# Attention and two dense layers on one core: narrower value weights, a new beginning, a new plan

## The chip, the core and the metric

The kernel runs on one core of a Trainium2 chip. The metric is the device time of one execution in microseconds (us). A core has TensorE (PE: matrix products; PEld in a profile is its weight load), VectorE (DVE), ScalarE (ACT), GpSimd (POOL) and SyncE (SP), which here issues nearly all transfers. Each engine works through its own queue in order; they wait for each other by semaphores.

## The reference

Inputs are q, k, v of shape (2, 8, 768, 64), a projection of 64x6, and the weights of two dense blocks.

```python
q_bits = (einsum('bhsd,dk->bhsk', q, proj) > 0)      # 6 bits, the same for k
mask = q_bucket[:, :, :, None] == k_bucket[:, :, None, :]
scores = where(mask, 0.125 * q @ k.T, -1e9); scores -= max(scores, -1)
attn = exp(scores); attn = attn / (sum(attn, -1) + 1e-9)
x = (attn @ v) laid out as 1536 tokens x 512
x = max(0.01 * (x @ w_in), x @ w_in) @ w_out          # 512 -> 2048 -> 512
h = x @ w_in2; return (h * cos(h)) @ w_out2           # 512 -> 2048 -> 512
```

The dense weights arrive as 64-bit floats.

## The kernel before

Every operand of a product is split into a high part and a low rest, and a product is the sum of high x high, high x low and low x high. Attention goes head by head (16 of them, n), within a head by tiles of 128 keys (six, k). Pieces of a head, by the names of the code: `load` and `hi`/`lo` split q and k into a tile `at` (four in a ring, so `at_71` holds heads 3, 7, 11 and 15); `bm`/`bw` are the bits product (L277) and its write (L283); `mm`/`mr` the products for row maxima (L293) and their reductions (L299); `rt`/`fl`/`dr` turn the maxima into a row, finish it and send it by DMA into `at` (L303, L308, L313); `qk` are the score products (L370, L371), `ex`/`cv` two passes of ScalarE over them, which give the exponential and its high part `phi`, `sub` the low rest `plo` (L392, on VectorE or GpSimd); `pe`, `pv`, `pw` the value products (L397, L405), which add up in one PSUM tile `pv`; `ev` copies it out, `lc`, `rc`, `dw`, `rr`, `xm` divide by the sum (its reciprocal is L419, and `lc`, L416, is the small DMA ahead of it). A value product has 128 weight columns: 64 of v, and 64 that are ones (for the sum of the row) on the other side for odd heads. The sum of v over all keys (`sv`, L342, with 65 columns of ones) enters the correction for rows without a match.

After the maxima of head n the row of -1 that goes with them was sent into each `at` once by a DMA (L454).

The dense weights are turned from 64-bit to two 32-bit floats in pieces `w0` to `w6` (L588 to L592 and L581; VectorE, ScalarE, GpSimd). The first eight chunks of them are placed among the last heads, since their space becomes free then. The two dense layers follow in 96 steps; the first twelve are part of the plan, the rest is written out.

The order of work is computed when the kernel is built: `Plan.order` keeps a time for each engine, takes for each engine the piece that can start first (ties go to the lowest key: `KEY` per kind, `FIX` for a kind and a head, `CHUNK_KEY`), adds its cost from `COST`, and so on. The resulting list is issued as it stands; each engine's queue is its share of that list.

## Time and profile before

| | us |
|---|---|
| three runs, median (lowest, highest) | 791.51 (790.81, 791.82) |
| span of the profiled execution, first to last instruction | 789.9 |
| TensorE busy in it | 772.2 |
| VectorE, ScalarE, GpSimd busy | 472.9, 435.1, 408.9 |

The profiled execution's own device time isn't listed apart from its span; the runs lie 0.9 to 1.9 us above the span, which begins with the first instruction and ends with the last. Busy time on TensorE counts a product from its start to its modelled end, so records of neighbours overlap, and a sum of durations is more than the time that passes. In a timeline a row in brackets with "idle" tells how long the engine stood before that group, and what ended the wait.

### The profile page before, as it was taken

To read this page: it belongs to the slowest core of one execution; us is meant where nothing else is said; L and a number is where in the kernel's file an instruction comes from. 1 tells how busy PE (TensorE), PEld (TensorE's weight loads), DVE (VectorE), ACT (ScalarE), POOL (GpSimd) and SP (SyncE) were. 2 spreads that over 40 slices of the span, in tenths; PEclk is the share of its full clock that TensorE was granted. 3 is DMA by queue.
4 is the path that set the end of the run, shared out by engine and by line. 5 is a ranking of instruction groups with operands and counts; after the bars stand their busy time and mean duration, and the time that the engine had idled before them with its cause. 6 is when DMAs were issued, how large, how long until landed. Compare 5 with 4: busy or idle time off the path is not lost.

```text
span 789.9 us, 9962 instructions
## 1 busy us (share of the span) xinstructions
PE 772.2 (98%) x3660; PEld 666.1 (84%) x3660; DVE 472.9 (60%) x599; ACT 435.1 (55%) x630; POOL 408.9 (52%) x263
## 2 busy tenths in 40 slices
PE   5999999999998999999999999999999999999998
PEld 3999999999888888888888888888888888888886
DVE  6656777777597875256366275357546738743333
ACT  3687777877778744243243233366556645644432
POOL 8777675666575634255345346747615433532211
PEclk9999999999999999999999999999999999999999
DMA  6553543542613622032022013112203200000012
GB/s 179 134 129 84 147 96 92 137 104 65 197 32 132 219 107 107 1 107 90 18 107 75 32 54 108 53 41 75 98 1 107 107 1 1 0 1 1 0 54 107
DMA packets 24329, 63.20 MB, mean 80 GB/s; under 512 B 7596, under 2 KB 11620, under 8 KB 20184
## 3 DMA queue, kind: packets, MB, share of 16 engines
q1 hardware_dynamic: 24136, 62.43, 26.0%
q8 instruction: 29, 0.48, 0.3%
q14 instruction: 20, 0.16, 0.1%
q10 hardware_dynamic: 144, 0.13, 0.0%
HBM read 46.21 MB, written 3.19 MB: 63 GB/s over the span
## 4 chain that ended last, share of the span: by engine, by line
PE 92%; DVE 3%; ACT 2%; DMA 2%; issue 1%; POOL 0%; SPq 0%; DVEq 0%; ACTq 0%; POOLq 0%
PE h L664 33%; PE y L706 33%; PE pv L405 11%; PE st L293 4%; PE st L370 4%; PE st L371 4%; PE st L277 2%; PE st L342 1%; DMA raw<-in_qk_dram 1%; PE pv L397 1%; DMA sums<-yx 1%; DVE mx L299 0%; ACT st L385 0%; DVE wsc L591 0%; ACT phi L377 0%
## 5 line engine op out<-in xcount | busy, mean ns | idle before, releaser
L695 POOL TENSOR_TENSOR gl<-gf,gh 128x512 fp32r<-128x512 f32 x88 | 136.2, 1548 | 261.1 <-ACT gh L689 188.7
L706 PE MATMUL y<-gh,at 128*128 128x512 f32 x576 | 177.0, 388 | 0.0
L664 PE MATMUL h<-XH,at 128*128 128x512 f32 x576 | 142.3, 389 | 0.0
L664 PEld LDWEIGHTS h<-XH,at 128*128 128x128 f32 x576 | 108.1, 188 | 22.4
L706 PEld LDWEIGHTS y<-gh,at 128*128 128x128 f32 x576 | 108.0, 188 | 22.4
L299 DVE TENSOR_REDUCE mx<-st 128x1 fp32r<-128x768 f32 x96 | 90.3, 953 | 37.1 <-PE st L293 35.3
L706 PE MATMUL y<-gl,at 128*128 128x512 f32 x288 | 111.8, 388 | 0.0
L392 POOL TENSOR_TENSOR plo<-pf,phi 128x768 fp32r<-128x768 f32 x43 | 81.3, 1894 | 56.1 <-ACT phi L388 49.3
L671 ACT ACTIVATE gf<-h 128x512 f32<-128x512 f32 x48 | 28.7, 597 | 139.8 <-PE h L664 135.8
L681 DVE TENSOR_TENSOR gf<-h,gf 128x512 f32<-128x512 f32 x48 | 33.2, 691 | 108.2 <-ACT gf L671 108.0
L675 ACT ACTIVATE ki<-h 128x512 int32<-128x512 f32 x48 | 28.7, 598 | 105.1 <-PE h L664 105.1
L676 DVE SCALAR_TENSOR_TENSOR gf<-ki,h 128x512 f32<-128x512 int32 x48 | 33.0, 687 | 75.1 <-ACT ki L675 75.1
L664 PE MATMUL h<-XL,at 128*128 128x512 f32 x288 | 77.0, 389 | 0.0
L370 PE MATMUL st<-at 77*128 77x384 f32 x192 | 67.0, 349 | 3.3 <-DVE plo L392 1.3
L371 PE MATMUL st<-at 128*128 128x384 f32 x192 | 65.1, 339 | 0.0
L585 POOL TENSOR_TENSOR at<-wsc,at 128x1024 fp32r<-128x1024 f32 x24 | 59.1, 2462 | 9.6 <-ACT at L592 9.6
L664 PEld LDWEIGHTS h<-XL,at 128*128 128x128 f32 x288 | 54.1, 188 | 11.2
L706 PEld LDWEIGHTS y<-gl,at 128*128 128x128 f32 x288 | 54.0, 188 | 11.1
L689 ACT ACTIVATE gh<-gf 128x512 fp32r<-128x512 f32 x96 | 60.0, 625 | 3.0 <-DVE gf L681 1.5
L706 PE MATMUL y<-gh,wx 128*128 128x512 f32 x192 | 58.7, 387 | 0.0
L685 DVE SCALAR_TENSOR_TENSOR gf<-gf,h 128x512 f32<-128x512 f32 x48 | 32.9, 686 | 41.7 <-ACT gf L684 41.7
L392 DVE TENSOR_TENSOR plo<-st,phi 128x768 fp32r<-128x768 f32 x53 | 50.3, 952 | 10.5 <-ACT st L385 9.1
(105 smaller groups left out, 1452.1 us busy)
## 6 DMA issues: line engine op xcount, KB each, us to landing
wrvh<-in_w_dram SPq DMA_DIRECT2D x16, 1024.0 KB
wrvl<-in_w_dram SPq DMA_DIRECT2D x16, 1024.0 KB
at<-at SPq DMA_DIRECT2D x63, 192.0 KB
raw<-in_qk_dram SPq DMA_DIRECT2D x15, 384.0 KB
vraw<-in_v_dram SPq DMA_DIRECT2D x4, 768.0 KB
yx<-dr SPq DMA_DIRECT2D x16, 192.0 KB
out_dram<-ys SPq DMA_DIRECT2D x6, 256.0 KB
out_dram<-yx SPq DMA_DIRECT2D x5, 256.0 KB
```

The lines of the kernel that those rows point to most:

```text
L299: V.reduce_max(mx[n][:, t:t + 1], mps.pop((n, t))[:, :, 0:HS], axis=AX.XY)
L370: T.matmul(o, at[0:R76 + 1, 2, kc], at[0:R76 + 1, 0, COL[h]], start=True, stop=False)
L371: T.matmul(o, at[:, 3, kc], at[:, 1, COL[h]], start=False, stop=True)
L392: (V if LO[n][k] == "V" else G).tensor_tensor(halves(plo[n, k]), pf.pop((n, k)), halves(f32(phi[n, k])), op=ALU.subtract)
L405: T.matmul(ot[n][:, h, 0:HS], w, x[:, COL[h]], start=False, stop=(k == C - 1 and part == 1))
L585: G.tensor_tensor(lf, sc, f32(hf), op=ALU.subtract)
L664: self.tc.nc.tensor.matmul(ps, w[:, 0, k], x[:, k, cols], start=(j == 0), stop=(j == 3 * KT - 1))
L676: nc.vector.scalar_tensor_tensor(g, ki, -TWOPI, ps, op0=ALU.mult, op1=ALU.add)
L681: nc.vector.tensor_tensor(g, ps, g, op=ALU.max)
L689: self.tc.nc.scalar.activation(gh, self.gs[s], AF.Copy)
L695: (nc.vector if s < GLV else nc.gpsimd).tensor_tensor(gl, g, f32(gh), op=ALU.subtract)
L706: self.tc.nc.tensor.matmul(self.half(e, c), w[:, 1, e], x[:, c], start=(j == 0 and i == 0), stop=(j == GRP - 1 and i == 2))
```

## The change

Value products get 65 weight columns: v's 64 and one of ones, so the sum always stands in row 64. The tiles `vh` and `vl` are laid out as 65 columns per head; the last factor of odd heads gets a tile of its own (`rr1`). The row of -1 comes as a 13th row with the key bits (threshold and weight in `cst`), and its four DMAs are gone. The signed projection is spread out on the host and finished by three VectorE steps; its two loads are issued by ScalarE. SyncE now issues the two halves of head 0, then v, then head 1. Clearing of `e` and `sv` goes from GpSimd to VectorE. `Plan` gets a second kind of dependence (`behind`: after a piece's start), a latency per engine apart from the cost (`TAIL`), other costs and other keys. 70 pieces `un` with the lowest priority are put on TensorE: each is a product of `ones` and `e0` into the first value tile, which nobody reads; the plan takes one where nothing else can start.

```diff
-    load=-181, hi=20, d2=-40, d3=51, lo=-43, dl=-14, bm=-37, bw=7, db2=-47, db1=-61, mm=-8, mr=34, rt=-30,
+    load=1353.52, hi=10.36, d2=366, d3=385.48, lo=1205.02, dl=-630.48, bm=-1032.92, bw=280.97, db2=-59.3,
...
-    mm=0.351, mr=0.953, rt=0.12, fl=0.55, dr=0.75, de=1.3, neg=0.65, qk=0.702, ex=0.81, cv=0.84, subV=0.95, subG=1.87,
+    mm=0.349, mr=0.87, rt=0.06, fl=0.43, dr=0.78, de=1.55, qk=0.704, ex=0.705, cv=0.735, subV=0.875, subG=1.81,
...
+TAIL = dict(P=0.16, V=0.09, A=0.1, G=0.05, Q=0.0)
+COLD = 7.0
+UNREAD = 70
...
-            if e == "P" and t < 22:
+            if e == "P" and t < COLD:
                 c *= 1.9
...
+            for o in it["behind"]:
+                o["left"] -= 1
+                o["at"] = max(o.get("at", 0.0), t)
+                if o["left"] == 0:
+                    ready[o["e"]].append(o)
+            end = t + c + TAIL[e]
...
-        SV = [con.tile([128, 4, 128], F32R, name=f"sv{i}") for i in range(2)]
+        SV = [con.tile([128, 4, DV], F32R, name=f"sv{i}") for i in range(2)]
...
+        A.dma_start(px, proj)
+        A.dma_start(cs, cst)
...
+        for i in range(2):
+            V.memset(f32(E[i]), 0.0)
+            V.memset(f32(SV[i]), 0.0)
+        signed = px[:, 0:BM]
+        V.tensor_tensor(signed, signed, px[:, BM:], op=ALU.mult)
+        V.tensor_copy(PB[0], signed)
+        V.tensor_tensor(PB[1], signed, f32(PB[0]), op=ALU.subtract)
...
         def pv_e(n):
             ot[n] = plan.tile("pv")
             for h in range(2):
-                T.matmul(ot[n][:, h, 0:HS], SV[(n // 4) % 2][:, n % 4, :], E[n % 2][:, COL[h]], start=True, stop=False)
+                T.matmul(ot[n][0:DV, h, 0:HS], SV[(n // 4) % 2][:, n % 4, :], E[n % 2][:, COL[h]], start=True, stop=False)
 
         def pv(n, k, part):
-            g, pr, par = (n // 4) % 2, (n % 4) // 2, n % 2
-            vh, vl = (t[g][:, k, pr].rearrange("p a d -> p (a d)")[:, par * 64:par * 64 + 128] for t in (VH, VL))
+            vh, vl = (t[(n // 4) % 2][:, k, n % 4, :] for t in (VH, VL))
...
-        def minus_one(n):
-            Q.dma_start(f32(AT[n][R76:R76 + 1, 2]), neg)
...
+        idle_ps = plan.tiles["pv"][0]
+        for i in range(UNREAD):
+            plan.add(("un", i), "P", "un", 9e5 + i, lambda: T.matmul(idle_ps[0:DV, 0, 0:256], ones, E[0][:, 0:256], start=True, stop=True),
+                     behind=[("un", i - 1)])
...
+        VH, VL = ([xp.tile([128, wn], I64, name=f"{t}{i}", tag=f"{t}{i}").bitcast(F32R)[:, 0:C * 4 * DV].rearrange("p (c h d) -> p c h d", c=C, h=4)
+                   for i in range(2)] for t in ("vh", "vl"))
...
-        plan = Plan(rings, dict(P=5.5, V=5.9, A=4.6, G=4.8, Q=3.6))
+        plan = Plan(rings, dict(P=1.8, V=4.0, A=2.8, G=0.8, Q=0.75))
```

The rest of `KEY`, all of `CHUNK_KEY`, and `FIX` (from 50 entries to some 430) change as the first two lines do. Three places show what this makes of the queues. Rows give line, operation, target and sources; lines after the change are those of the changed file (L536 unread, L355 bits, L371 maxima, L446 and L447 scores, L480 values, L468 `sub`, L377 `mr`, L664 to L666 and L656 weight steps).

TensorE's first rows before: bits of head 0 (`at_68`), then its maxima.

```order
L277 MATMUL st_108<-at_68,pb_123 108x384
L277 MATMUL st_108<-at_68,pb_124 108x384
L277 MATMUL st_108<-at_68,pb_123 108x384
L277 MATMUL st_109<-at_68,pb_123 108x384
L277 MATMUL st_109<-at_68,pb_124 108x384
L277 MATMUL st_109<-at_68,pb_123 108x384
L293 MATMUL st_110<-at_68 128x384 x2
L293 MATMUL st_108<-at_68 128x384 x2
L293 MATMUL st_109<-at_68 128x384 x2
L293 MATMUL st_110<-at_68 128x384 x2
```

And after, with the unread products between.

```order
L536 MATMUL pv_112<-e_97,ones 65x256 x14
L355 MATMUL st_109<-at_68,pb_121 109x384
L355 MATMUL st_109<-at_68,pb_122 109x384
L355 MATMUL st_109<-at_68,pb_121 109x384
L355 MATMUL st_110<-at_68,pb_121 109x384
L355 MATMUL st_110<-at_68,pb_122 109x384
L355 MATMUL st_110<-at_68,pb_121 109x384
L536 MATMUL pv_112<-e_97,ones 65x256 x19
L371 MATMUL st_111<-at_68 128x384 x2
L371 MATMUL st_109<-at_68 128x384 x2
L371 MATMUL st_110<-at_68 128x384 x2
```

Fourteen products now stand ahead of the first bits product and nineteen ahead of the maxima; the other 37 stand among and behind the maxima. The first of them waits for `e_97` (E0), which VectorE clears and GpSimd fills.

ScalarE's first activations before: two halves of head 0, its keys' copy (L464), a bit copy (L451), head 1, the other bit copy, v.

```order
L443 ACTIVATE at_68<-raw_85 128x384 x2
L464 ACTIVATE at_68<-at_68 64x768
L451 ACTIVATE at_68<-at_68 12x384
L259 ACTIVATE at_69<-raw_86 128x768
L451 ACTIVATE at_68<-at_68 12x384
L331 ACTIVATE vh_72<-vraw_87 128x6x2x64 x2
L259 ACTIVATE at_70<-raw_85 128x768
```

And after (L528 is the bit copy, L337 a head, L409 v).

```order
L520 ACTIVATE at_68<-raw_86 128x384 x2
L542 ACTIVATE at_68<-at_68 64x768
L409 ACTIVATE vh_72<-vraw_88 128x6x2x64
L528 ACTIVATE at_68<-at_68 13x384
L337 ACTIVATE at_69<-raw_87 128x768
L528 ACTIVATE at_68<-at_68 13x384
L409 ACTIVATE vh_72<-vraw_88 128x6x2x64
L337 ACTIVATE at_70<-raw_86 128x768
```

A half of v has moved ahead of the first bit copy; the copy of head 1 stands between the two as before.

TensorE around the last maxima of head 15 (`at_71`) before; `at_70` is head 14, and the rows of L405 are value products.

```order
L303 MATMUL st_108<-ident,mx_107 6x128
L293 MATMUL st_110<-at_71 128x384 x2
L293 MATMUL st_109<-at_71 128x384 x2
L293 MATMUL st_108<-at_71 128x384 x2
L405 MATMUL pv_111<-plo_92,vh_73 128x384 x2
L405 MATMUL pv_111<-phi_89,vh_73 128x384 x2
L405 MATMUL pv_111<-phi_89,vl_75 128x384 x2
L293 MATMUL st_110<-at_71 128x384 x2
L370 MATMUL st_109<-at_70 128x384
L371 MATMUL st_109<-at_70 128x384
L370 MATMUL st_109<-at_70 128x384
L371 MATMUL st_109<-at_70 128x384
```

And after, the end of the same maxima up to the row product of head 15 (L381).

```order
L371 MATMUL st_109<-at_71 128x384 x2
L446 MATMUL st_111<-at_70 128x384
L447 MATMUL st_111<-at_70 128x384
L446 MATMUL st_111<-at_70 128x384
L447 MATMUL st_111<-at_70 128x384
L371 MATMUL st_110<-at_71 128x384 x2
L480 MATMUL pv_112<-plo_94,vh_73 65x384 x2
L446 MATMUL st_109<-at_70 128x384
L447 MATMUL st_109<-at_70 128x384
L446 MATMUL st_109<-at_70 128x384
L447 MATMUL st_109<-at_70 128x384
L381 MATMUL st_110<-ident,mx_106 6x128
```

Before, maxima products stand in groups ahead of the score products of head 14; after, each pair of them is followed by score products.

VectorE at the same place before: reductions of head 15 (`mx_105`), subtractions (`plo`), weight steps (`wsc`).

```order
L299 TENSOR_REDUCE mx_105<-st_110 128x1
L299 TENSOR_REDUCE mx_105<-st_109 128x1
L299 TENSOR_REDUCE mx_105<-st_108 128x1
L299 TENSOR_REDUCE mx_105<-st_110 128x1
L591 SCALAR_TENSOR_TENSOR wsc_77<-wrvh_1886,wsc_77 128x1024
L392 TENSOR_TENSOR plo_93<-st_109,phi_90 128x768
L581 SCALAR_TENSOR_TENSOR wsc_77<-wrvh_1886,wsc_77 128x1024
L392 TENSOR_TENSOR plo_91<-st_108,phi_89 128x768
L419 RECIPROCAL sums<-sums 128x6
L308 TENSOR_SCALAR mt_101<-st_110 6x128
```

And after (`mx_106` is head 15).

```order
L493 RECIPROCAL sums<-sums 128x6
L377 TENSOR_REDUCE mx_106<-st_109 128x1
L666 SCALAR_TENSOR_TENSOR wsc_79<-wrvl_1921,wsc_79 128x1024
L377 TENSOR_REDUCE mx_106<-st_110 128x1
L377 TENSOR_REDUCE mx_106<-st_109 128x1
L656 SCALAR_TENSOR_TENSOR wsc_79<-wrvl_1921,wsc_79 128x1024
L468 TENSOR_TENSOR plo_93<-st_111,phi_90 128x768
L377 TENSOR_REDUCE mx_106<-st_110 128x1
L377 TENSOR_REDUCE mx_106<-st_109 128x1
L377 TENSOR_REDUCE mx_106<-st_110 128x1
L386 TENSOR_SCALAR mt_102<-st_110 6x128
L387 TENSOR_SCALAR mt_102<-st_110 6x128
```

Two weight steps now stand among the reductions, and a reciprocal ahead of them. In SyncE's queue the small DMA that this kind of reciprocal waits for (`sums<-yx`) stands directly behind a weight load four times after the change; before, once directly and once with three DMAs between.

## Rows read from the trace of the kernel before

**Rows 1.** the page: its first line and the busy line (us, share of the span, instructions):

```profile
span 789.9 us, 9962 instructions
...
PE 772.2 (98%) x3660; PEld 666.1 (84%) x3660; DVE 472.9 (60%) x599; ACT 435.1 (55%) x630; POOL 408.9 (52%) x263
```

**Rows 2.** chain of waits, three runs of equal products: start us, us, what, count:

```profile
226.23 1.74 PE pv L405 x10
...
37.93 1.15 PE st L342 x10
...
777.47 0.36 PE h L706 x3
```

**Rows 3.** stretches: window and length, busy us and count per engine, PEclk, DMA, GB/s:

```profile
0.00:30.00 30.00, 20.95 (x76) 15.86 (x77) 19.28 (x34) 13.69 (x19) 21.56 (x48) 1.00 0.68 184
30.00:200.00 170.00, 169.67 (x965) 163.53 (x964) 120.74 (x159) 131.77 (x177) 115.09 (x64) 1.00 0.43 106
200.00:263.70 63.70, 59.11 (x308) 53.93 (x307) 50.71 (x57) 49.70 (x64) 39.88 (x21) 0.97 0.37 119
263.70:786.00 522.30, 522.30 (x2316) 432.82 (x2315) 281.31 (x349) 239.94 (x372) 232.42 (x133) 1.00 0.17 60
```

**Rows 4.** timeline of TensorE: start us, us, engine, line, operation, form, count, [idle before]:

```profile
6.10 0.62 PE L277 MATMUL st<-at,pb 128*108 128x384 f32 x1 [6.10 <-DVE pb L230]
...
19.53 0.41 PE L342 MATMUL st<-vh,ones 128*65 128x256 f32 x1
19.75 0.41 PE L342 MATMUL st<-vl,ones 128*65 128x256 f32 x1
...
23.34 0.34 PE L370 MATMUL st<-at 77*128 77x384 f32 x1
23.52 0.34 PE L371 MATMUL st<-at 128*128 128x384 f32 x1
```

**Rows 5.** weight loads by line: duration in ns min/median/max, first and last start:

```profile
L342 PEld LDWEIGHTS st<-vh,ones x24: 134/135/231, 17.8 to 177.1; 128*65 128x65 f32 x24
...
L405 PEld LDWEIGHTS pv<-plo,vh x192: 186/188/330, 29.7 to 263.2; 128*128 128x128 f32 x192
```

**Rows 6.** timeline of GpSimd, one row of E0 being filled:

```profile
4.83 0.73 POOL L242 MEMSET e<- 1x768 f32 x1
```

**Rows 7.** timeline of SyncE: halves of head 0, v, a row maximum:

```profile
2.00 1.06 SPq L216 DMA_DIRECT2D raw<-in_qk_dram  x2
...
8.90 0.63 SPq L325 DMA_DIRECT2D vraw<-in_v_dram  x1
...
18.46 0.74 SPq L313 DMA_DIRECT2D at<-mt  x1
```

**Rows 8.** timeline of ScalarE: head 0, bit copy, head 1, v:

```profile
4.60 1.13 ACT L443 ACTIVATE at<-raw 128x384 fp32r<-128x384 f32 x2 [2.57 <-DMA raw<-in_qk_dram]
...
9.44 0.52 ACT L451 ACTIVATE at<-at 12x384 fp32r<-12x384 f32 x1 [2.84 <-DVE at L283]
9.98 0.84 ACT L259 ACTIVATE at<-raw 128x768 fp32r<-128x768 f32 x1
...
14.69 1.58 ACT L331 ACTIVATE vh<-vraw 128x768 fp32r<-128x768 f32 x2 [3.32 <-DMA vraw<-in_v_dram]
```

**Rows 9.** timeline of VectorE: reductions of head 0, bits of head 1:

```profile
12.14 5.28 DVE L299 TENSOR_REDUCE mx<-st 128x1 fp32r<-128x768 f32 x6 [1.90 <-PE st L293]
...
18.66 1.09 DVE L283 TENSOR_SCALAR at<-st,cs 44x768 fp32r<-44x768 f32 x1
```

**Rows 10.** two stretches late in the attention part:

```profile
215.00:240.00 25.00, 21.58 (x114) 18.91 (x112) 23.92 (x25) 18.87 (x25) 17.52 (x9) 1.00 0.18 54
240.00:245.00 5.00, 4.79 (x18) 4.79 (x19) 3.39 (x7) 3.41 (x5) 2.75 (x2) 0.66 0.35 112
```

**Rows 11.** timeline of VectorE around the stop near 236 us:

```profile
232.47 3.55 DVE L299 TENSOR_REDUCE mx<-st 128x1 fp32r<-128x768 f32 x4
235.94 3.35 DVE L591 SCALAR_TENSOR_TENSOR wsc<-wrvh,wsc 128x1024 int32<-128x1024 int32 x1
```

More of the change, by code (lines that the diff above doesn't have):

```diff
@@ L83 @@
 R76 = 64 + 2 * NB
-BM = 96 + 2 * NB
+BM = 96 + 2 * NB + 1
+DV = D + 1
 def f32(ap):
@@ L105, in tile, with add @@
         return self.tiles[ring][self.place]
-    def add(self, name, e, kind, key, fn, after=(), take=None, give=(), cost=None, moe=False):
+    def add(self, name, e, kind, key, fn, after=(), take=None, give=(), cost=None, moe=False, behind=()):
         deps = [self.index[d] for d in after if d is not None and d in self.index]
+        ahead = [self.index[d] for d in behind if d in self.index]
         it = dict(name=name, e=e, kind=kind, key=(key, len(self.items)), fn=fn, deps=deps, take=take, give=list(give),
-                  cost=COST[kind] if cost is None else cost, out=[], left=len(deps), moe=moe, before=[], place=0)
+                  cost=COST[kind] if cost is None else cost, out=[], left=len(deps) + len(ahead), moe=moe, before=[], place=0, behind=[], ahead=ahead)
         for d in deps:
             d["out"].append(it)
+        for d in ahead:
+            d["behind"].append(it)
         self.items.append(it)
@@ L169, in order @@
                 o["left"] -= 1
-                o["at"] = max(o.get("at", 0.0), end + LAT[o["e"]] * (o["e"] != e or e == "Q"))
+                o["at"] = max(o.get("at", 0.0), end + LAT[o["e"]] if e != "P" or o["e"] != e else t + c)
                 if o["left"] == 0:
@@ L175, in order, with attention @@
         return done
-def attention(tc, ctx, plan, sums, dr_p, XH, XL, AT, VH, VL, YX, qkt, v, proj, cst, fd, more_raws, heads=NH):
+def attention(tc, ctx, plan, sums, dr_p, XH, XL, AT, VH, VL, YX, rr1, qkt, v, proj, cst, fd, more_raws, heads=NH):
     nc = tc.nc
@@ L404, in pv @@
                 for h in range(2):
-                    T.matmul(ot[n][:, h, 0:HS], w, x[:, COL[h]], start=False, stop=(k == C - 1 and part == 1))
+                    T.matmul(ot[n][0:DV, h, 0:HS], w, x[:, COL[h]], start=False, stop=(k == C - 1 and part == 1))
             if part:
@@ L760, in do @@
             def do(kind, e, fn, *args, j=(), after=(), take=None, give=(), cost=None):
-                plan.add((kind, s) + tuple(j), e, kind, key + KEY[kind], lambda: fn(*args), after, take, give, cost, moe=True)
+                plan.add((kind, s) + tuple(j), e, kind, key + FIX.get((kind, s), KEY[kind]), lambda: fn(*args), after, take, give, cost, moe=True)
             x = [("xl", n) for n in range(1, H if b == 0 else NH, 2)]
@@ L867 @@
     ins["v"] = a["v"].reshape(B, H, C, 128, D).transpose(0, 3, 2, 1, 4)
-    ins["proj"] = a["proj"]
+    ins["proj"] = np.zeros((128, 2 * BM), np.float32)
+    for s in range(2):
+        for j in range(2):
+            c0 = 64 + 32 * s + j * NB
+            ins["proj"][64 * s:64 * s + 64, c0:c0 + NB] = a["proj"]
+            ins["proj"][64 * s:64 * s + 64, BM + c0:BM + c0 + NB] = 1.0 if s == j else -1.0
     for p, m in (("moe_", "w1"), ("moe2_", "w2")):
```

140 lines of the change are left out of this document (57 added, 83 removed), and 96 rows, old and new, of the table FIX.

## The prediction

> **What bounds the kernel now.** I read the page's busy line first: the span is 789.9 us and TensorE is busy for 772.2 of it (98%) [rows 1]. So an edit counts only if it takes work off TensorE, closes a gap between its products, or makes it run faster. "Busy" hides two losses, since a product's record is longer than the distance to the next one. So I take distances from the chain of waits [rows 2]: ten value products (weights 128x128, 384 columns) take 1.74 us, 0.174 each; ten 256-column products with 65 weight columns take 1.15, 0.115 each; three 256-column products with 128 weight columns take 0.36, 0.120 each. Times the counts of each stretch [rows 3], the work that TensorE would need without a loss is:
> - 0 to 30 us: 76 products, 12 of them the 256-column sums: 64 x 0.175 + 12 x 0.115 = 12.6; lost 17.4.
> - 30 to 200: 965, of them 36 sums and 12 short row products (0.06): 917 x 0.175 + 36 x 0.115 + 0.7 = 165.3; lost 4.7.
> - 200 to 263.7: 308 x 0.175 = 53.9; lost 9.8.
> - 263.7 to 786 (the two dense layers): busy 522.30 of 522.30; lost nothing.
>
> All the loss, 32 us, is in the attention part, over half of it in the beginning. There the timeline of TensorE [rows 4] shows the first product at 6.10 us, and 256-column products that start 0.21 us apart (19.53, 19.75): 256 columns at 1.2 GHz, though the clock column of [rows 3] shows 1.00 for this stretch. The first score product starts at 23.34 and the next at 23.52: 0.18 for 384 columns, so the full 2.4 GHz was there by then and not at 19.75.
>
> **Part 1: 65 weight columns in value products.** 16 heads x 6 key tiles x 6 products and 32 products that open a sum are 608 products with 65 instead of 128 weight columns; the moving columns stay 384. Lower bound: no gain, if the distance doesn't depend on the weights. Upper bound: 384 columns at 2.4 GHz are 0.160 us, so at most 0.0145 of the 0.174 can go, 8.8 us in all. The nearest row is the one pair with equal columns: 0.120 against 0.115, 5 ns at most with the rounding; 608 x 0.004 = **2.4 us**, my value.
>
> The shorter weight loads themselves (135 against 188 ns [rows 5]) gain nothing: they run beside the product before.
> The Trainium skill ("TensorE: Matmul & The Clock Gate", Weight-path perf modes) speaks against this part: it says that the fast weight load is on only for 128 weight columns, and not for FP32. By that rule 65 columns would lose a fast load and these products would get slower. The trace disagrees so far: a 128-column load takes longer than a 65-column one, as if neither were fast. It is a rival below.
>
> **Part 2: the new beginning.** It no longer sends four rows of -1 through SyncE, prepares the signed weights in 3 VectorE steps instead of 10, loads v ahead of all other heads, moves clearing from GpSimd to VectorE, and puts 70 products that nobody reads into TensorE's queue. I follow its first chain by durations of before. All starts here are estimates from those rows.
> - The unread products read E0, so they wait until it is cleared and filled. A 1x768 row took GpSimd 0.73 [rows 6]; no row shows VectorE clearing that much, so I bound each of its two clears by the same. They start near 0.8 and end at about 0.8 + 1.46 = 2.3, and GpSimd's two rows of E0 behind them at 3.8. So 14 unread products at 0.21 run from 3.8 to 6.7, and the first bits product, queued behind them, waits that long though its data (the first half of head 0 was with ScalarE 2.6 us after its issue began, at 2.00 and 4.60; then 0.57 for the copy and as much for the subtraction [rows 7, 8]; the issue is now two issues sooner, near 0.8) would be there at about 4.5. That costs up to 2.2 us if nothing covers it.
> - Something does. ScalarE has a half of v's conversion ahead of the first copy of the key bits, and the load of head 1 ahead of the second. v took from 9.53 (its issue's end) to 14.69 [rows 7, 8], 5.2 us; issued third by SyncE, until about 2.4, it lands at 7.6. Then 0.79 + 0.52 + 0.84 + 0.52 [rows 8]: the last bit copy ends at 10.3, and the maxima products of head 0 start then. The bits products (6 x 0.175 from 6.7) and VectorE's two bit writes (together at most the 1.09 and a start more [rows 9]) are done before each copy asks for them.
> - Six reductions on VectorE took 5.28 [rows 9]; from 10.7 they end at 16.0, against 12.14 + 5.28 = 17.42 before. Then the same engine writes the bits of head 1 (1.09, to 17.1) and a part of the sum of v before it finishes the row maxima; I allow 1.4 for that, the time of the 12 sum products ahead of it on TensorE (12 x 0.115): 18.5. The row DMA takes from issue to use what head 0's first half took, 2.6, and 0.2 more for its longer issue (0.74 [rows 7]): 21.3, and the first score product starts there, against 23.34.
> - By then TensorE has done two more maxima products (0.35). Gain 23.34 - 21.3 + 0.35 = **2.4 us**. Bounds: -1 (the row DMA as late as before and the clock at half for the first 12 us) and +6 (all that lies at half pace, about 40 products x 0.17).
>
> The 70 products cost 8.1 us of TensorE at 0.115, all of it in gaps: 14 before the first bits product, 56 while VectorE reduces and the row DMA flies. Without that cover it is 8.1 us.
>
> **Part 3: the new plan.** It issues the same work in another order, so its price is how much of the 4.7 and 9.8 us stays.
> - Late stretch: from 215 to 245, 132 products x 0.175 = 23.1 of 30 us: 6.9 of the 9.8 are lost here, with the granted clock at 0.66 from 240 to 245 [rows 10], which is 3.4 us at the lower level, after a stop. VectorE reduces head 15's maxima in one row of four (3.55 us), then runs a weight step of 3.35 us before the subtraction for which TensorE waits [rows 11]. In the old order four maxima products of head 15 stand ahead of head 14's score products. In the new one each stands between score products of heads 13 and 14, so ScalarE has exponentials to do meanwhile; two weight steps go between the first three of the six reductions, and two stand side by side only at the very end, where four did. These stops go, and about a quarter returns elsewhere: **5.5 us**. Bounds: -5 (the same number of stops somewhere else) and 9.8.
> - Middle: many short waits, none named. The same rebalancing should take a quarter of 4.7: **1.2 us**; bounds -4.7 and 4.7.
> - Next late after the stops: the dense part's weights. The low half of the fourth chunk comes after the first dense products; TensorE has three input products and one output product of 12 x 0.226 each (10.8 us; 522.3 / 2316 [rows 3]) ahead of it, and I see some 10 us of steps. I cost it at nothing; if the cover fails it costs 1 to 3 us.
>
> **Sum.** 2.4 + 2.4 + 5.5 + 1.2 = 11.5. Span 789.9 - 11.5 = 778.4; about 1.6 us lie around the profiled span (median 791.5 of the runs against it), so **780.0 us**. Its own range is 775 to 785.
>
> **Rivals.**
> - *The order gains nothing* (784 to 788): the losses after 30 us stay at 14.5, in other places. For it: VectorE and ScalarE were busy 96% and 75% of 215 to 240 [rows 10], so any order is tight. Against: the two longest stops have a cause that the order removes. 791.5 - 4.8 = 786.7.
> - *The unread products don't lift the clock*, and the bits products and the 19 unread ones behind them run at half pace: 6 x 0.35 + 19 x 0.21 puts the maxima at 12.8 instead of 10.3; the start then gains nothing: 791.5 - 9.1 = 782.4.
> - *The order packs the attention almost without loss*: 2.4 + 2.4 + 11 gives 775.7. For it: the dense part already runs 522 us without a gap.
> - *Fast weight load lost*: the 15 ns by which 0.175 exceeds its columns' time doubles; 608 x 0.015 = 9.1 lost in place of 2.4 gained: 780.0 + 11.5 = 791.5.
> - *Slower: VectorE stands at the reciprocal.* Each head's reciprocal waits for a small DMA which in the new SyncE order stands right behind a 1 MB weight load four times (before: once, and once with three DMAs between). VectorE's queue behind it then holds maxima and subtractions. The reciprocal's DMA behind such a load would land some 3.4 us late (1 MB at the 5.2 us that v's 0.75 MB took, shared with nothing else: up to 7); four stands of 3.4 and one fall of the clock (1.7, half of 3.4 us at half pace) cost 15 in place of the 6.7 gained: 791.5 - 4.8 + 15 = 802. It makes the kernel slower once two stands cost TensorE their full length. Against: other VectorE work is placed ahead of each.
>
> **Chances.** Forecast 0.60, no gain from order 0.16, clock not lifted 0.06, nearly no loss 0.09, fast load lost 0.03, stands 0.06. A measurement of this kernel tells 0.2% (1.6 us) from no change: faster means under 789.9. Forecast, first three rivals and a little of the rest: 0.90; same 0.04; slower 0.06. The range 771 to 788 holds the forecast, the two fast-side rivals and most of the first.
>
> **What would show it.** Full pace (0.175 per 384 columns) from the first maxima product at about 10, the first score product near 21, value products 4 ns closer together, loads of 135 ns, no drop of the granted clock near 240, last attention product near 252. The prediction is wrong if value products are not closer together, if the first score product comes after 23, or if VectorE waits for the reciprocal's DMA while TensorE stands.

## The result: 784.9 us against 791.7 us, and the profile after

The changed kernel takes 784.88 us (median of 4 runs, 783.94 to 787.20) against 791.66 for the kernel before on the same chip: ratio 0.991, 95% interval 0.9885 to 0.9935. Run again beside other kernels it took 784.69 against 791.96, ratio 0.9908 (0.9882 to 0.9933). The gain is some 7 us; 11.5 were forecast.

The page of the profiled execution (785.27 us) answers to [rows 1]:

```profile
span 783.2 us, 10076 instructions
...
PE 770.2 (98%) x3730; PEld 648.8 (83%) x3730; DVE 479.7 (61%) x594; ACT 433.5 (55%) x630; POOL 401.0 (51%) x240
```

TensorE is busy for the same 98%, with 70 products more. The share can't tell a busy TensorE from a useful one; the stretches can. They answer to [rows 3], columns as there, with the end of the attention part at 256.9 instead of 263.7:

```profile
0.00:30.00 30.00, 24.13 (x141) 22.29 (x142) 18.02 (x29) 12.02 (x17) 12.88 (x24) 0.94 0.64 174
30.00:200.00 170.00, 169.89 (x984) 150.18 (x983) 123.67 (x160) 135.21 (x183) 117.63 (x65) 1.00 0.44 112
200.00:256.90 56.90, 53.60 (x294) 43.34 (x293) 48.65 (x54) 46.41 (x60) 40.67 (x20) 1.00 0.39 122
256.90:779.00 522.10, 522.10 (x2314) 432.64 (x2313) 288.14 (x351) 239.89 (x372) 229.88 (x133) 1.00 0.16 59
```

The dense part is as long as before (522.1 against 522.3), so the whole difference of 6.7 us lies in the attention part. I count what each stretch loses as the prediction does: its length less the products that start in it, 0.175 per 384 columns, 0.115 per 256, nothing for an unread one. All numbers are counted from the starts in the traces with the same stretches (200 to 270 takes the beginning of the dense part in), so those of before differ a little from the prediction's 17.4, 4.7 and 9.8:

| lost, us | 0 to 30 | 30 to 200 | 200 to 270 | sum |
|---|---|---|---|---|
| before | 17.5 | 5.0 | 10.4 | 33.0 |
| after | 18.4 | 1.7 | 6.3 | 26.4 |
| change | +0.9 | -3.3 | -4.1 | -6.6 |
| forecast (65 columns apart: -2.4) | -2.4 | -1.2 | -5.5 | -9.1 |

So in this trace the beginning got worse, and everything came from the stretches behind it. Where a loss falls differs from trace to trace: 1.7 us of the 18.4 are a fall of the clock (below), and experiment 3, which has the same beginning, lost 16.7 there without such a fall, but 3.4 between 30 and 200. The sum up to 200 is steadier: 19.7 to 21.3 in the five traces with this order and this beginning, or nearly (after, after again, experiments 2 to 4), against 22.5 in before. TensorE's beginning, in its timeline (L536 unread, L355 bits, L371 maxima, L446 first score product):

```profile
3.84 3.25 PE L536 MATMUL pv<-e,ones 128*65 128x256 f32 x14 [3.84 <-POOL e L329]
6.88 1.50 PE L355 MATMUL st<-at,pb 128*109 128x384 f32 x6
8.22 2.40 PE L536 MATMUL pv<-e,ones 128*65 128x256 f32 x19
11.41 0.44 PE L371 MATMUL st<-at 76*128 76x384 f32 x1 [0.79 <-ACT at L528]
12.84 1.16 PE L371 MATMUL st<-at 76*128 76x384 f32 x5 [0.98 <-ACT at L528]
...
15.99 2.01 PE L355 MATMUL st<-at,pb 128*109 128x384 f32 x6
...
22.08 2.52 PE L536 MATMUL pv<-e,ones 128*65 128x256 f32 x20
24.43 0.86 PE L371 MATMUL st<-at 76*128 76x384 f32 x4
25.13 0.34 PE L446 MATMUL st<-at 77*128 77x384 f32 x1
```

The bits at 6.88 are as worked out (6.7). Then two stops, each for a bit copy of ScalarE (L528), and the first score product at 25.13: 1.8 us later than before [rows 4], where 21.3 was forecast. ScalarE tells why (L409 converts v, L337 copies head 1), against [rows 8]:

```profile
9.96 0.85 ACT L409 ACTIVATE vh<-vraw 128x768 fp32r<-128x768 f32 x1 [4.17 <-DMA vraw<-in_v_dram]
10.84 0.52 ACT L528 ACTIVATE at<-at 13x384 fp32r<-13x384 f32 x1
11.40 0.84 ACT L337 ACTIVATE at<-raw 128x768 fp32r<-128x768 f32 x1
12.27 0.52 ACT L528 ACTIVATE at<-at 13x384 fp32r<-13x384 f32 x1
```

ScalarE stood 4.17 us for v, whose load took 7.6 us from the end of its issue (2.34) to its first use instead of the 5.2 that I took from before. The first bit copy stood behind that, though both copies had their own data at 9.3 (VectorE's two bit writes, 7.99 and 1.29 long). The second copy stood behind the copy of head 1 as well, and head 1's load was there only at 11.38, as the chain of waits says (columns as in [rows 2]):

```profile
2.38 9.00 DMA raw<-in_qk_dram
```

So the second copy, and with it the maxima at 12.84, would have come no sooner if v alone had landed at 7.6. VectorE next, against [rows 9] (L361 bits of head 0, L377 reductions, L361 bits of head 1, L386 row maxima), and SyncE's row DMA:

```profile
7.99 1.29 DVE L361 TENSOR_SCALAR at<-st,cs 45x384 fp32r<-45x384 f32 x2 [1.67 <-PE st L355]
13.32 3.55 DVE L377 TENSOR_REDUCE mx<-st 128x1 fp32r<-128x768 f32 x4 [4.05 <-PE st L371]
18.40 1.82 DVE L377 TENSOR_REDUCE mx<-st 128x1 fp32r<-128x768 f32 x2 [1.53 <-PE st L371]
20.26 1.09 DVE L361 TENSOR_SCALAR at<-st,cs 45x768 fp32r<-45x768 f32 x1
...
22.41 0.28 DVE L386 TENSOR_SCALAR mt<-st 6x128 f32<-6x128 f32 x1
```

```profile
22.71 0.73 SPq L391 DMA_DIRECT2D at<-mt  x1
```

The six reductions start 2.6 us late and have a hole of 1.53 in them: on TensorE the bits of head 1 (15.99) stand ahead of the last four maxima products and run at half pace, 0.32 us apart. That is the granted clock, in the third column from the right here:

```profile
8.00:14.00 6.00, 4.22 (x30) 3.62 (x29) 1.95 (x3) 3.92 (x6) 3.04 (x2) 1.00 0.67 169
14.00:18.00 4.00, 4.00 (x19) 3.81 (x17) 2.88 (x4) 0.40 (x1) 3.87 (x3) 0.57 0.94 234
18.00:30.00 12.00, 11.74 (x80) 10.74 (x79) 8.83 (x12) 4.52 (x7) 2.21 (x2) 1.00 0.49 134
```

Full (2.4 GHz) from 8 to 14, 0.57 from 14 to 18, so nearly all of it at 1.2 GHz, behind the two stops for the copies, at a cost of 1.7 us (0.43 of 4); full again from 18. What ran before the clock's first rise this column doesn't show: it says 1.00 for the first 30 us of before too, where 256-column products were 0.21 apart at 19.75 [rows 3, 4]. Here the first 14 unread products are 0.217 apart (3.84 to 6.88) and those from 8.22 on 0.117. Late, the two stretches of [rows 10] have become:

```profile
215.00:240.00 25.00, 22.87 (x125) 18.54 (x125) 22.02 (x25) 20.05 (x26) 21.08 (x11) 1.00 0.34 111
240.00:245.00 5.00, 5.00 (x31) 4.26 (x30) 4.05 (x4) 5.00 (x8) 4.26 (x3) 1.00 0.18 44
```

125 products instead of 114 in the same 25 us, 31 instead of 18 in the next 5, and no drop of the clock. Of the value products the chain of waits says (columns as in [rows 2]; above them a sum of v), and below it their loads:

```profile
42.98 1.43 PE st L420 x12
...
224.91 2.79 PE pv L480 x16
```

```profile
L480 PEld LDWEIGHTS pv<-phi,vl x192: 134/135/139, 30.3 to 254.9; 128*65 128x65 f32 x192
```

Sixteen in 2.79 us: 0.174 each, to a nanosecond or two the same as with 128 columns (experiment 3 has the finer count), although their loads take 135 ns instead of 188 [rows 5].

### The profile page after: what moved, and what is told of

Same layout as the page of the kernel before. It is cut to its first block, busy times and chain, and to the rows that moved or that the text cites. A ratio compares the mean times of both kernels' runs of the same rounds, so it can differ in the third digit from the quotient of the medians.

```text
span 783.2 us, 10076 instructions
## 1 busy us (share of the span) xinstructions
PE 770.2 (98%) x3730; PEld 648.8 (83%) x3730; DVE 479.7 (61%) x594; ACT 433.5 (55%) x630; POOL 401.0 (51%) x240
## 4 chain that ended last, share of the span: by engine, by line
PE 94%; DMA 2%; DVE 2%; issue 1%; ACT 1%; SPq 0%; DVEq 0%; ACTq 0%
PE h L739 33%; PE y L781 33%; PE pv L480 11%; PE st L371 4%; PE st L446 4%; PE st L447 4%; PE st L355 2%; DMA raw<-in_qk_dram 1%; DMA sums<-yx 1%; PE st L420 1%; PE pv L536 1%; PE pv L473 1%; DVE mx L377 0%; DVE plo L468 0%; DVE wsc L666 0%
## 5 line engine op out<-in xcount | busy, mean ns | idle before, releaser
L377 DVE TENSOR_REDUCE mx<-st 128x1 fp32r<-128x768 f32 x96 | 90.6, 954 | 33.0 <-PE st L371 31.9
L468 POOL TENSOR_TENSOR plo<-pf,phi 128x768 fp32r<-128x768 f32 x43 | 81.6, 1903 | 52.7 <-ACT phi L464 43.6
L446 PE MATMUL st<-at 77*128 77x384 f32 x192 | 65.8, 343 | 1.3 <-DVE plo L468 1.0
L764 ACT ACTIVATE gh<-gf 128x512 fp32r<-128x512 f32 x96 | 59.9, 624 | 10.4 <-DVE gf L756 5.4
L447 PE MATMUL st<-at 128*128 128x384 f32 x192 | 64.9, 338 | 0.0
L468 DVE TENSOR_TENSOR plo<-st,phi 128x768 fp32r<-128x768 f32 x53 | 50.5, 954 | 16.2 <-ACT st L461 15.4
```

What stands on the lines that cost most here:

```text
L377: V.reduce_max(mx[n][:, t:t + 1], mps.pop((n, t))[:, :, 0:HS], axis=AX.XY)
L446: T.matmul(o, at[0:R76 + 1, 2, kc], at[0:R76 + 1, 0, COL[h]], start=True, stop=False)
L447: T.matmul(o, at[:, 3, kc], at[:, 1, COL[h]], start=False, stop=True)
L468: (V if LO[n][k] == "V" else G).tensor_tensor(halves(plo[n, k]), pf.pop((n, k)), halves(f32(phi[n, k])), op=ALU.subtract)
L764: self.tc.nc.scalar.activation(gh, self.gs[s], AF.Copy)
```

## The experiments

All ratios are to the kernel before, measured beside the run, with their 95% intervals.

**1. No unread products** (the kernel after without its 70; every engine's order kept).

```diff
-                it["fn"]()
+                if it["name"][0] != "un":
+                    it["fn"]()
```

> The changed kernel without its 70 unread products, every other instruction in the same order. Theory 1 (they lift TensorE's clock early, and that is worth something): without them products up to about 22 us run 0.35 apart instead of 0.175, the sums of v take 2.5 us instead of 1.45, the first score product comes 1.5 to 3 us later than 25.1, and the time is 786.5 to 788 against 784.9. Theory 2 (they only stand in the way: the beginning is gated by ScalarE and by DMAs): the first score product comes at 25 or earlier and the time is 783 to 785.

791.05 us, ratio 0.9993 (0.9976 to 1.0009): without them the whole gain is gone, more than either theory said. Its trace has lost 2.2 us more than after's at 35 us and 3.6 in all (its profiled execution, 789.02, was the soonest of its 12), so that some 3 of the 6.6 us between the ratios stand in no trace. The stop ahead of the first score product, and the granted clock:

```profile
24.02 0.95 PE L371 MATMUL st<-at 76*128 76x384 f32 x4 [1.66 <-DMA at<-at]
```

```profile
18.00:25.00 7.00, 4.56 (x28) 3.88 (x27) 5.25 (x8) 0.75 (x2) 0.00 (x0) 1.00 0.36 87
25.00:32.00 7.00, 7.00 (x23) 6.29 (x23) 3.91 (x5) 4.63 (x6) 4.00 (x3) 0.52 0.78 230
```

The first score product comes even sooner (24.80 against 25.13), but behind a stop of 1.66 us for a DMA, which 20 unread products fill in the kernel after, and from 25 on the score products run at half pace, 0.32 apart, for some 7 us. As far as the trace shows it, the first theory is right that half pace costs the gain, but not where: the sums of v (19.6 to 21.1) run at full pace, 0.12 apart. None of its 12 executions had a mean granted clock above 0.998; of 10 of the kernel after five had 1.000.

**2. Bit copies ahead of v** (ScalarE's queue only).

```diff
-hi.0  vh.0.0  kb0.0  hi.1  kb0.1  vh.0.1
+hi.0  kb0.0  kb0.1  vh.0.0  hi.1  vh.0.1
```

> The changed kernel with one move on ScalarE: both bit copies of head 0 ahead of the first half of v (and so ahead of head 1). Theory 1 (the first maxima product came at 12.84 because the second bit copy stood behind v and head 1, whose loads landed at 9.96 and 11.38): the maxima start at 10 to 10.7, the row maximum is finished some 2 us earlier, the first score product comes near 23, the time is 782.5 to 783.3. Theory 2 (what gates the first score product is further on: v's low parts, the bits of heads 1 and 2): the maxima start earlier, the first score product stays within 0.5 us of 25.1, and the time within 0.5 us of 784.9.

784.51 us, ratio 0.9914 (0.9892 to 0.9935): the same time as after. In the trace the maxima come at 10.88, near the 10.3 of the prediction:

```profile
10.88 1.23 PE L371 MATMUL st<-at 76*128 76x384 f32 x6
...
14.98 0.95 PE L355 MATMUL st<-at,pb 128*109 128x384 f32 x4 [0.99 <-POOL at L341]
...
23.60 0.34 PE L446 MATMUL st<-at 77*128 77x384 f32 x1
```

The first score product comes at 23.60, not far from the 23 of theory 1, but the time is that of theory 2. One stop of 0.99 us is left, for the low part of head 1 (L341), whose load again came at 11.4, and the clock never falls (a mean of 1.000 in all 6 executions):

```profile
14.00:18.00 4.00, 3.02 (x21) 2.86 (x22) 2.67 (x4) 0.76 (x2) 4.00 (x3) 1.00 0.88 217
```

1.6 us less is lost by 30 us, 1.2 of it is given back until 200 (2.9 against 1.7), and 0.5 won behind. The end is 0.9 us sooner in one trace, less than the runs can tell.

**3 and 4. Weight columns: 128 again, and 65 laid 80 apart** (order unchanged).

```diff
-T.matmul(ot[n][0:DV, h, 0:HS], w, x, ...)        # w: 65 columns
+T.matmul(ot[n][:, h, 0:HS], w, x, ...)           # w: 128 columns, read on into the next head
```

```diff
-VH, VL: [:, 0:C * 4 * DV] as (c, h, d=65)
+VH, VL: [:, 0:C * 4 * 80] as (c, h, 80), of which 65 are read
```

> The changed kernel with 128 weight columns in all 608 value products (each reads on into the next head's columns; the extra 63 output rows are not read), same order of work. Theory 1 (columns of the weights do not set the distance of these products): distances stay at 0.175 and the time within 0.7 us of the changed kernel's. Theory 2 (the prediction's term): 0.004 us more per product, 2.4 us more. Theory 3 (a fast load that only 128 columns get): shorter distances, 1 us less or better.

> The changed kernel with the 65 weight columns of each head laid out 80 columns apart (320 bytes) instead of 65 (260 bytes), same order of work. Theory 1 (the gain of 65 columns was lost to weights that start at odd addresses): value products 0.171 apart, loads shorter, time 2 to 2.5 us less than the changed kernel's. Theory 2 (the distance is set by the moving columns and does not depend on the weights): distances 0.175, time within 0.5 us.

785.74 us (0.9927, 0.9903 to 0.9951) and 784.55 us (0.9913, 0.9891 to 0.9934). The chain of waits of the kernel with 128 columns has the same row as that of after:

```profile
224.37 2.79 PE pv L484 x16
```

That row is too coarse for a nanosecond. Over all pairs of value products that start directly one behind the other (from 45 to 235 us, up to 0.186 us apart, 387 to 407 pairs in a trace) the mean distance is 174.7 ns in after and in experiment 4, 175.9 with 128 columns here and 176.3 in before: 1.2 to 1.6 ns, which makes 0.7 to 1.0 us over 608 products (an estimate). The medians are 0.9 us apart, which the intervals can't tell from zero. So experiment 3 lies between its first two theories, nearer to the first, and experiment 4 fits its second: where the columns lie doesn't matter.

Experiment 3 shows one thing more. It has the beginning of the kernel after, and in its trace the clock doesn't fall there:

```profile
12.54 1.16 PE L374 MATMUL st<-at 76*128 76x384 f32 x5 [1.11 <-ACT at L532]
...
23.34 0.34 PE L449 MATMUL st<-at 77*128 77x384 f32 x1
```

```profile
14.00:18.00 4.00, 4.00 (x30) 3.75 (x29) 3.98 (x5) 0.10 (x1) 3.46 (x3) 1.00 0.96 237
```

One stop of 1.11 us where after has 0.79 and 0.98, no fall, and the first score product at 23.34: 1.8 us sooner than in after, and just when it comes in before [rows 4].

**5 to 8. Beginning, order and unread products crossed.** The planner is given each engine's queue as a list of names, so that a kernel keeps its own beginning up to the first score product (and the few pieces that surround it on the other engines) and has the other kernel's order from there on. The old beginning gets 61 unread products on a tile of its own.

```diff
-ts = [(start(it), it) for it in ready[e]]
-...
+turn = [it for it in ready[e] if name_of(it) == QUEUES[e][at[e]]]
```

> The kernel before with its own beginning (no unread products, 128 weight columns, v loaded late); from the first score product on, every engine's queue stands in the order of the kernel after. Theory 1 (the two parts add: the new order saves some 7.5 us after 30 us, as the losses of the two traces say, 5.0 + 10.4 against 1.7 + 6.3): 791 - 7.5 = 783.5, about the time of the kernel after, with losses near 17.5 in the first 30 us, 2 from 30 to 200 and 6 behind. Theory 2 (the gain hangs on the unread products, since the kernel after without them ran in 791): 790 to 792.

> As the run of the old beginning with the new order, and 61 unread products of 256 columns in the old beginning (26 ahead of the first bits product, 8 behind the bits, 19 between the maxima, 8 ahead of the sum of v), on a tile of their own that VectorE clears first. Theory 1 (they lift the clock wherever TensorE would stand, and the old beginning has its products at half pace until about 21.5): bits, maxima and sums of v run at full pace, the first score product comes at 22 or sooner against 23.34, and the time is 2 to 5 us under the run without them: 778 to 781, under the kernel after. Theory 2 (the unread products only repair what the new beginning does badly): within 1 us of the run without them.

> The kernel after with its own beginning, unread products and 65 columns; from the first score product on, every engine's queue stands in the order of the kernel before. Theory 1 (the order carries the gain, the new beginning with its unread products is 1 us worse than the old one): 791 to 793, with the loss of 230 to 245 us and the drop of the granted clock near 240 back. Theory 2 (the unread products carry it): 785 to 786, as the kernel after.

> The kernel before, whole, with the same 61 unread products in its beginning and nothing else changed. Theory 1 (the parts add): what the unread products give in the old beginning, 2 to 5 us: 786 to 789. Theory 2 (the unread products carry the whole gain): 785. If the old beginning hides its slow products behind VectorE and the row DMA, 790 to 791.

| beginning | unread | order | us | ratio to before (interval) | lost 0 to 30, to 200, to 270 |
|---|---|---|---|---|---|
| old | no | old (before) | 793.3 beside these | 1 | 17.5, 5.0, 10.4 |
| old | no | new (5) | 788.99 | 0.9961 (0.9938 to 0.9984) | 20.3, 5.4, 5.7 |
| old | yes | new (6) | 788.83 | 0.9951 (0.9929 to 0.9973) | 17.0, 5.2, 5.8 |
| new | yes | old (7) | 789.31 | 0.9960 (0.9944 to 0.9976) | 18.1, 4.5, 7.3 |
| old | yes | old (8) | 789.64 | 0.9966 (0.9943 to 0.9988) | 20.7, 5.8, 7.2 |
| new | no | new (1) | 791.05 | 0.9993 (0.9976 to 1.0009) | 19.6, 4.0, 6.4 |
| new | yes | new (after) | 784.88 | 0.9910 (0.9885 to 0.9935) | 18.4, 1.7, 6.3 |

The rows come from different chips, with before at 790.9 beside (1), 791.7 beside after and 793.3 beside 5 to 8, so I compare ratios, not times. For 5 and 7 neither theory holds: the new order alone gives 3.1 us (0.0039 x 791), not 7.5, and not nothing; the new beginning with its unread products (and the 65 columns) gives 3.2 under the old order, not -1 and not the whole 6.5. For 6 the second holds, since 788.83 is within 1 us of 788.99, and for 8 the first at its lower end, 2.7 us. The two halves, 3.1 and 3.2, add to 6.3, and together they measure 7.1, the same within the intervals, which reach some 1.8 us to either side. So behind the new beginning the new order is worth 4.0 us (0.9960 to 0.9910) and behind the old one 3.1, which these runs can't tell apart. The unread products are worth 6.6 us in the new beginning (0.0083), but 0.8 to 2.7 in the old one; without them the new beginning is 2.5 us worse than the old (0.9993 against 0.9961). In the traces the new order loses as little as 1.7 between 30 and 200 only behind the beginning that it was planned with (2.2 to 3.4 in experiments 2 to 4); behind the old one it loses 5.2 to 5.4, no less than the old order. Late it loses 5.7 to 6.4 behind either (7.2 to 7.3 for the old order in the two traces without a fall of the clock near 240), so that part belongs to the order.

One trace for each kernel is a sample, and the old beginning's differ: ScalarE's first conversion of v starts at 14.69 in the trace of before [rows 8], at 15.09, 16.01 and 17.97 in those of kernels 6, 5 and 8, the same load from the same place in the queue, 5.2 to 8.4 us after its issue ended at 9.53. The latest, in kernel 8:

```profile
17.97 1.58 ACT L432 ACTIVATE vh<-vraw 128x768 fp32r<-128x768 f32 x2 [6.60 <-DMA vraw<-in_v_dram]
```

The clock differs too: 21 of 82 executions of before had a mean granted clock of 1.000 and some 790.5 us, 16 one of 0.996 and some 795. Executions at 1.000 were 8 of 12 for kernel 5 (median 788.3 us), 5 of 10 for kernel 7 (788.7) and 5 of 10 for the kernel after (784.5). So either half of the change makes the low ones rarer, and among executions at 1.000 the gain is 6.0 us.

**9. The first 14 unread products alone.** The other 56 are left out of TensorE's queue.

```diff
-un x14  bm0.0 bm0.1  un x19  mm.0.0 ...
+un x14  bm0.0 bm0.1  mm.0.0 ...
```

> The kernel after with only the first 14 of its 70 unread products (those ahead of the first bits product); order otherwise unchanged. Theory 1 (the clock is lifted by the first 14, but falls again in the gaps that the other 56 would have filled): full clock from 7.5, then half again between 14 and 32, mean clock 0.995 to 0.998, time 787 to 790. Theory 2 (once lifted by the 14 it stays up): 784 to 785. Theory 3 (14 products do nothing by themselves): 790 to 791.5, as without any.

791.06 us, ratio 0.9986 (0.9966 to 1.0005), which can't be told from none at all: the time is the third theory's, the course of the clock the first's. It goes up, falls, goes up and falls again:

```profile
9.00:12.00 3.00, 0.44 (x1) 0.19 (x1) 0.67 (x1) 1.69 (x3) 1.19 (x1) 1.00 0.84 196
12.00:19.00 7.00, 5.87 (x17) 4.91 (x17) 3.89 (x5) 2.74 (x4) 5.75 (x4) 0.51 0.75 183
19.00:25.50 6.50, 4.28 (x27) 3.71 (x27) 5.28 (x8) 0.75 (x2) 0.00 (x0) 1.00 0.35 85
25.50:32.00 6.50, 6.50 (x22) 5.70 (x21) 3.41 (x5) 4.63 (x6) 3.85 (x3) 0.52 0.74 229
```

Ahead of the second and the fourth stretch TensorE stood for 2.6 of 3 and for 2.2 of 6.5 us. So the worth of the unread products lies in the gaps that they fill until the score products run, not in raising the clock once. The other 56 without these 14 were not run. The mean clock (0.987 to 0.995) is lower than without any unread product (0.995 to 0.998) at the same time, because it leaves out what runs before the first rise, which comes before 12 here and near 18 without any.

**10. The kernel after again**, for its spread.

> The kernel after, unchanged, beside the next two on one chip, so that they can be set against it and its granted clock seen over several executions. Theory 1 (part of its time is a draw of the clock in the first 25 us, since maxima products wait for ScalarE's late bit copies): executions between 783.5 and 787.5, the mean granted clock between 0.996 and 1.000, ratio to before near 0.991. Theory 2 (its time is fixed by its order): all executions within 1 us at one clock.

784.69 us, executions from 782.87 to 785.38, four at a clock of 1.000 (median 784.3), the others at 0.997 and 0.999. The ratio and the clocks are those of the first theory. But the four at 1.000 alone spread over 2.5 us (782.87 to 785.35), so the draw of the clock, worth about 1 us here, is not most of the spread; what the rest is stays open.

**11. A beginning after the prediction's own chain.** Bit copies first; all maxima of head 0 ahead of the bits of head 1; row maxima ahead of those bits on VectorE; the row DMA five DMAs sooner; the first score product ahead of head 1's maxima.

```diff
 TensorE
-mm.0.3 un bm.1 mm.0.4 un mm.0.5 un sv.0 bm.2 rt.0 un x20 mm.1.0 mm.1.1 qk.0.0
+mm.0.3 un mm.0.4 un mm.0.5 un bm.1 rt.0 sv.0 un x12 qk.0.0 bm.2 qk.0.1 mm.1.0 mm.1.1
 VectorE
-mr.0.5 bw.1 sl.0 fl.0
+mr.0.5 fl.0 bw.1 sl.0
 GpSimd
-vl.0.0 lo.1 vl.0.1
+lo.1 vl.0.0 vl.0.1
 SyncE
-d3.2 d2.2 dl.2 db1.1 db2.1 dr.0 db1.2 db2.2 load.3 de.0
+d3.2 dr.0 db2.1 d2.2 db1.1 dl.2 db1.2 db2.2 load.3 de.0
```

> The kernel after with another beginning, same work: ScalarE copies both halves of the key bits before it converts v; TensorE has all twelve maxima products of head 0 ahead of the bits of head 1, and the first score product ahead of head 1's maxima; VectorE finishes head 0's row maxima right behind their reductions; SyncE issues the row DMA five DMAs sooner; 62 unread products in place of 70, 12 instead of 19 of them ahead of the maxima. Theory 1 (the beginning is a chain: copies, six reductions, row maxima, row DMA): maxima at 10.2, row DMA issued at 17 to 18 instead of 22.7, first score product at 20.5 instead of 25.1, 2 to 3 us less lost before 35 us, time 781.5 to 783. Theory 2 (behind the first score product VectorE and ScalarE set the pace, so what TensorE gains there it loses before 60 us): 784 to 785, as the kernel after.

The kernel has 57 unread products, not 62. 790.11 us, ratio 0.9976 (0.9956 to 0.9996), slower than after. The chain itself came out as expected or sooner, and then TensorE stood (rows of its timeline: a stop in the sum of v, the first score product, then the product that opens head 0's sum):

```profile
17.30 0.34 PE L518 MATMUL st<-vl,ones 128*65 128x256 f32 x1 [1.64 <-POOL vl L511]
...
20.07 0.34 PE L544 MATMUL st<-at 77*128 77x384 f32 x1
...
28.51 0.87 PE L571 MATMUL pv<-e,sv 128*65 128x384 f32 x2 [2.41 <-DMA e<-mt]
```

Five microseconds sooner at the first score product, 2.5 us less lost at 25 us than after, and by 35 us 2.3 more. The sum row's DMA (`de.0`) and the load of head 3 still stood at the end of SyncE's list, behind head 2's DMAs, which wait for VectorE. The product that needs the sum row waited 2.41 us, and from 27 to 34 the granted clock was 0.51:

```profile
15.00:27.00 12.00, 8.38 (x52) 7.21 (x51) 6.73 (x10) 3.23 (x5) 5.79 (x4) 1.00 0.55 126
27.00:34.00 7.00, 5.49 (x18) 4.88 (x19) 1.22 (x3) 4.41 (x6) 4.00 (x3) 0.51 0.77 231
```

Behind the stop of 1.64 us it had stayed full. Neither theory said that: it was an order of SyncE that fitted the old place of the first score product.

**12. The same with SyncE's queue mended** and 12 more unread products. The diff is against experiment 11.

```diff
 TensorE
-rt.0 sv.0 un x12 qk.0.0
+rt.0 un x14 sv.0 un x10 qk.0.0
 SyncE
-d3.2 dr.0 db2.1 d2.2 db1.1 dl.2 db1.2 db2.2 load.3 de.0
+d3.2 d2.2 dr.0 db2.1 de.0 load.3 db1.1 dl.2 db1.2 db2.2
```

> The kernel with the other beginning (first score product at 20.07 in its trace), with SyncE's queue mended: the sum row's DMAs and the load of head 3 stand right behind the row DMA and the key-bit DMA of head 1 instead of behind head 2's, head 2's second copy ahead of them, and 69 unread products, 14 of them now in the gap ahead of the sum of v. Theory 1 (its loss of 5.6 us between 25 and 35 us, with the granted clock at half from 27.2 to 34.0, came from TensorE's stop of 2.41 us for the sum row's DMA): no stop over 1 us behind the first score product, clock full from 7 on, 15.5 to 16 us lost by 35, time 781.5 to 783.5, under the kernel after. Theory 2 (VectorE and ScalarE can't follow an earlier first score product, whatever SyncE does): stops of the same sum in other places, clock at half again, 786 to 790.

789.38 us, ratio 0.9952 (0.9934 to 0.9971); no better than the kernel after either. The time is the second theory's, but not for its reason: the stop moved to the unread products themselves:

```profile
22.88 0.87 PE L635 MATMUL pv<-e,ones 128*65 128x256 f32 x3 [2.68 <-DMA e<-mt]
```

They read `e0`, and the sum row's DMA, now ahead of the last three of them in the program, writes it. So they waited for it, with the score products queued behind. From 22 to 29 the clock was 0.52:

```profile
22.00:29.00 7.00, 6.12 (x21) 6.03 (x21) 1.11 (x2) 2.38 (x4) 1.81 (x1) 0.52 0.45 123
```

Whether an earlier first score product, without either mistake, beats the kernel after was not tried again and stays open. No kernel here beat it by more than the runs can tell.

## Why the prediction was right in sign, and where its steps failed

- **What bounds the kernel**: right. TensorE stayed at 98%, the dense part didn't move (522.1), and the 6.7 us came from the attention part's losses alone.
- **65 weight columns, -2.4**: mis-sized. The 4 ns priced (a pair 0.120 against 0.115) aren't there: the starts show 1.2 to 1.6 ns, 0.7 to 1.0 us over the 608, and the times can't tell even that from zero. The pair that I took for it stood in different places: in the trace of after the same 65-column sums are 0.119 apart, 12 in 1.43 us. Nor do 65 columns slow the product down, so the rival in which a fast load is lost falls too. The Trainium skill's rule behind it ("TensorE: Matmul & The Clock Gate", Weight-path perf modes: a fast load only for 128 columns, not for FP32) is not contradicted: the 128-column loads took 188 ns, so there was no fast one to lose.
- **New beginning, -2.4**: the failed step is the landing of the loads: "v lands at 7.6", and, without a word, head 1 in time for its copy at 8.9. v was in ScalarE at 9.96 and head 1 came at 11.38; the second put the maxima's second half at 12.84 instead of 10.3. The 5.2 us of before was one draw: the same load took up to 8.4 in the old place (kernel 8), and 7.2 to 8.4 in seven traces of the new one (after, experiments 1, 3, 4, 7, 9 and 10). That the loads beside it slow it down is likely, but no run shows it. Of the 3.8 us by which the first score product is late (25.13 instead of 21.3) the start of the reductions makes 2.6 (13.32 instead of 10.7) and the hole in them 1.5, while the row DMA gives 0.4 back (2.4 instead of 2.8). The hole comes from the bits of head 1 between the maxima, which the prediction didn't follow. Loads and hole don't simply add: in experiment 2 the reductions start at 11.45, and the first score product still comes at 23.60; in experiment 3, with no hole and no fall of the clock, at 23.34 behind a start at 13.02. So 1.8 us of the 3.8 go with the fall of the clock, and 2 would have been missed without it.
- **Unread products**: the forecast saw in them 8.1 us of hidden work and priced their failure at 2.4 (782.4). Without them the gain is gone, 6.6 us by the ratios. The price missed what a stop costs after the beginning has ended: some 7 us at half pace at 25 us, where real products stand, each 0.145 us longer. That and the stops make 3.6 us in the trace; where the other 3 lie is open.
- **New plan, late, -5.5**: 4.1 in the traces. The drop near 240 is gone, as forecast, and the longest stop of TensorE behind 200 is 0.95 us instead of 1.32. But most of it hangs on that one fall of the clock in the trace of before: without one the old order loses 7.2 to 7.3 there (kernels 7 and 8), the new one 5.7 to 6.4, so only 0.8 to 1.6 us are the order's own. The fall itself is no rarity, since 43 of 82 executions of before had a mean clock of 0.998, that of its trace, or less; whether it comes at this place in them no trace shows.
- **New plan, middle, -1.2**: 3.3, and only behind its own beginning and with its unread products (1.7 against 4.0 without). The forecast took it for a property of the order; in the traces of the crossed kernels it belongs to order and beginning together. In experiments 2 and 3, where the clock doesn't fall before 30, the beginning loses 1.6 to 1.8 less and this stretch 1.2 to 1.8 more, so that much of the 3.3 only makes up for the fall.
- **Rivals**: "the order gains nothing" would have been 786.7, nearer to the time than the forecast, but not for its reason: the order gained (3.1 to 4.0 us by the ratios), and the columns and, in the trace, the beginning didn't give their 4.8. VectorE's waits for the reciprocals' DMA (waited for, total us, times, longest) are

```profile
DVE sums L493 <- DMA sums<-yx: 4.6, 7, 1.2
```

  and before they were 5.5 in 5, 2.1 at most; TensorE's waits name none of them, and no stop of 3.4 us came, so that rival is refuted. No run speaks for an order almost without loss.
- **The sum**: -11.5 forecast, -6.7 in the traces: 2.4 too much for the columns, 3.3 for the beginning, 1.4 for the late stretch, 2.1 too little for the middle; 2.4 + 3.3 + 1.4 - 2.1 = 5.0, of which 4.8 are seen. The little that the columns give lies within the stretches in this count.
- **Its own signs**: of the three that were to show it wrong one came, a first score product after 23, and one all but came, value products only 1.2 to 1.6 ns closer together instead of 4. That the time still lies in the range of 775 to 785, at its upper end, is partly luck: the middle stretch gave nearly three times its term.

## What to carry to other kernels

A DMA's time read once is not a price: the same load took 5.2 to 8.4 us in four traces. Cost it by such a range, do so for every load on the chain, and follow what is queued behind its consumer to the end. Where an engine slows down after a stop, price a stop by the pace of what comes after it as well as by its length, and a filler by the stops that it bridges; see to it that no late writer touches what the filler reads. An order planned by numbers is measured with the beginning that it was planned with and behind another: here the traces show its gain between 30 and 200 us only behind its own, while the runs (4.0 and 3.1 us) can't tell the two apart. And where one trace splits a gain into stretches, look at the same stretches of a second: what one lost by a fall of the clock, the next stretch made up for.

## What the runs showed of the hardware that was not expected

- The distance of products with 384 columns is 174.7 ns with 65 weight columns and 175.9 with 128 in the same order, though the loads take 135 and 188 ns.
- The granted clock fell behind stops of 0.79 and 0.98 us close together (0.57 from 14 to 18), of 1.66, 2.41 and 2.68 us (0.51 to 0.52 for some 7 us), but not behind a single one of 0.99 us in experiment 2, of 1.11 in experiment 3 or of 1.64 in experiment 11: the length of a stop alone doesn't tell. 14 products ahead of the real ones raised it, and it fell again within the next gap.
- One kernel draws different clocks in different executions: before has 790.5 us at a mean of 1.000 and some 795 at 0.996.
- The same load of v, issued by 9.53, was first used between 14.69 and 17.97 in four traces with the same queue ahead of it.
